# Attention steps split finer and each placed by hand, weights joined in four steps, and a reordered end, in a linear-attention and cosine-FFN kernel on one core

## The chip, the cores and the metric

The kernel runs on 1 core of one Trainium2 chip. The metric is device microseconds of one execution. Before the change the median of 3 runs is 587.07 us (585.82 to 587.1). Five engines work side by side, each in the order of its own instruction list: PE (matmuls, with the weight load PEld), DVE (elementwise, scans), ACT (activations), POOL (elementwise) and SP (issues transfers).

## The reference, cut to what matters

Two stages follow each other: a linear attention with decay over 768 steps, for 4 batches and 8 heads of 48, and a feed-forward stage on its output, seen as 3072 tokens of 384.

```python
for t in range(S):                         # attention, per batch and head
    cur = u * kt (outer) vt
    y[t] = rt @ (state + cur)
    state = wt[:, None] * state + kt (outer) vt
x = y as (B*S, H*D)                        # 3072 x 384
h = x @ w_in                               # 384 -> 2048
g = h * cos(h)
out = g @ w_out                            # 2048 -> 384
```

## The kernel before, in words

The time axis is cut into chunks of 128 steps, each of two halves of 64 (SUB); 4 batches of 6 chunks are 24 chunks (`j`), and two chunks of different batches form a block (BLK = 2), so there are 12 blocks. Attention in a chunk is done with matmuls: scores inside a half, a state carried from half to half.

The steps of a chunk or block, by the short names of the tables (before's lines):
- `load`, `lr`, `lv` (L195 to L214) issue the transfers of the transposed tile `tt` (112 x 1545: r, k, and the decays w), of `rk` and of `v`.
- `decay` (L216) is one step: `rkt` for the first six chunks, the suffix scan `ee` (L223), the running minimum `shrink` (L226), `whole` (L228), its reciprocal into `inj` (L229), the prefix scan into `tt` (L230), and r and k scaled by the two (L233, L234).
- `diag` (L236) makes `cd` and, on the engine that the table names for `asb`, the diagonal of the score tile (L255).
- `a`/`A` (L269) scores and the masked copy (L281), `t`/`T` (L283) transposes of k and the copy to `kn`, `s` (L303) states, `d` (L264) decayed states `dd`, `o` and `b` (L336) the own part of the output, `p` (L359) the past part, the copy `yf` and the transfers `xf<-yf` that turn the layout, `x` (L379) the split of `xf` into a high part (a cast) and a low part (a subtraction) `xT`.

The feed-forward runs in units: a block has 8 units of 256 hidden columns, 96 in all. `mm1` (L419) is 18 matmuls into a PSUM bank `ph`, then `gate` (L395): ACT L399, DVE L400, ACT L401 (sine) and L402 (square), DVE L403, then the cast `gh` to `gs` and two low parts `g0`, `g1` (L155). L403 is the last reader of the bank. `mm2` (L436) is 12 matmuls into the block's accumulators, up to LAG = 3 units behind mm1; after a block's last unit `ob` (L454) goes out.

Weights come as 64-bit words; `load_weights` (L164) makes a float from the two halves of a word and splits it into a high and a low part: ACT L174 and L176, DVE L178, L179 and L186, ACT the cast, DVE the low part (L155). This is done once for 16 pieces, during the first units.

What sets the order: `START` (L60) is a written list of steps up to block 2 with the units of blocks 0 and 1 between, `PLAN` (L52) the list that each later unit adds, 8 rows for the 8 units of a block; PE follows these lists as written. The other engines' order comes from a scheduler that goes by program order and its own costs. `EARLY` and `LATER` say which engine does what (v DVE, a ACT, p POOL, s SP). After the last unit a `vote` (L570) sums two checks in PSUM, every engine loads its result (L582), and a branch skips the fallback `one_by_one`.

## Time and profile before

| | us |
|---|---|
| median of the runs (3) | 587.07 |
| lowest, highest | 585.82, 587.1 |
| the profiled execution's own time | 586.22 |
| its span, first to last instruction | 584.5 |
| PE busy | 514.9 |
| DVE busy | 415.9 |
| ACT busy | 258.5 |
| POOL busy | 241.7 |
| mean granted TensorE clock | 0.977 of 2.4 GHz |

A busy time is the time in which at least one instruction of the engine ran. An engine takes its instructions in order, so an instruction that waits holds back all behind it. A releaser is what ended such a wait. PE is the busiest engine; its idle time shows in which stage another engine or a transfer sets the pace.

### The profile page before, as it was taken

The numbers are of one execution on the slowest core, as the hardware profiler recorded it, in microseconds if no ns is written. First come the engines' busy times: TensorE is split into PE (matmuls) and PEld (weight loads), VectorE is DVE, ScalarE is ACT, GpSimd is POOL, SyncE is SP. The second block draws the span as 40 slices with busy tenths as digits, with TensorE's granted clock in tenths as the row PEclk, the third lists the DMA queues.
The fourth block names the chain that finished last, engine by engine and source line by source line (L and its number), as shares of the span: only waits on it lengthen the run. The fifth ranks groups of instructions, "written<-read, shape, count | busy, mean of one in ns | idle before, by whom it ended". The sixth has DMA issues, their size and how long they took to land.

```text
span 584.5 us, 14459 instructions
## 1 busy us (share of the span) xinstructions
PE 514.9 (88%) x6084; PEld 489.4 (84%) x6084; DVE 415.9 (71%) x716; ACT 258.5 (44%) x445; POOL 241.7 (41%) x280
## 2 busy tenths in 40 slices
PE   1557588988889999899899999899899899999994
PEld 1447478877878989899899989899799899999994
DVE  6998999999586874964963965855854846945431
ACT  2435678843354253253353453353442443443541
POOL 2221443565445445453543635534543533243231
PEclk9999879999899999999999999999999899999998
DMA  8928354002432504305205207006015006401001
GB/s 280 333 68 295 113 181 153 24 33 82 138 105 93 130 2 144 88 29 148 58 29 150 56 29 192 13 29 178 1 32 148 1 28 194 160 31 27 27 1 34
DMA packets 21849, 56.37 MB, mean 96 GB/s; under 512 B 3088, under 2 KB 13968, under 8 KB 21776
## 3 DMA queue, kind: packets, MB, share of 16 engines
q1 hardware_dynamic: 19616, 53.59, 30.6%
q10 hardware_dynamic: 2160, 1.77, 1.4%
q8 instruction: 50, 0.82, 0.6%
q14 instruction: 23, 0.19, 0.1%
HBM read 45.91 MB, written 4.72 MB: 87 GB/s over the span
## 4 chain that ended last, share of the span: by engine, by line
PE 47%; DVE 34%; DMA 10%; issue 4%; ACT 2%; SPq 1%; POOL 1%; DVEq 0%; ACTq 0%
PE acc L445 21%; PE ph L431 19%; DMA xf<-yf 5%; DVE tt L230 5%; DVE ee L223 4%; DMA tt<-tr 3%; DVE rr L403 3%; DVE w L155 2%; DVE rr L400 2%; DVE h L179 2%; PE py L348 2%; DVE h L186 2%; PE py L367 2%; DVE shrink L226 2%; DVE h L178 1%
## 5 line engine op out<-in xcount | busy, mean ns | idle before, releaser
L155 POOL TENSOR_TENSOR gs<-rr,gs 128x256 fp32r<-128x256 f32 x192 | 164.5, 878 | 254.2 <-DVE gs L152 186.5
L431 PE MATMUL ph<-xT,w 128*128 128x256 f32 x1728 | 229.5, 288 | 23.4 <-DVE rr L403 14.6
L431 PEld LDWEIGHTS ph<-xT,w 128*128 128x128 f32 x1728 | 219.5, 194 | 28.9 <-issue 15.7
L445 PE MATMUL acc<-w,gs 128*128 128x384 f32 x1152 | 221.5, 343 | 5.4 <-ACT gs L152 3.6
L445 PEld LDWEIGHTS acc<-w,gs 128*128 128x128 f32 x1152 | 198.2, 189 | 9.7 <-ACT gs L152 4.0
L401 ACT ACTIVATE rr<-rr 128x512 f32<-128x512 f32 x96 | 60.7, 632 | 162.7 <-DVE rr L400 162.6
L400 DVE SCALAR_TENSOR_TENSOR rr<-rr,ph 128x512 f32<-128x512 int32 x96 | 65.1, 678 | 49.0 <-ACT rr L399 49.0
L403 DVE SCALAR_TENSOR_TENSOR rr<-rr,ph 128x512 f32<-128x512 f32 x96 | 65.4, 682 | 41.0 <-ACT rr L402 39.9
L399 ACT ACTIVATE rr<-ph 128x512 int32<-128x512 f32 x96 | 56.8, 591 | 82.0 <-PE ph L431 68.6
L402 ACT ACTIVATE rr<-rr 128x512 f32<-128x512 f32 x96 | 60.6, 632 | 2.6
L223 DVE TENSOR_TENSOR_SCAN ee<-tt,one_e 112x520 f32<-112x520 f32 x24 | 35.3, 1472 | 24.9 <-DMA tt<-tr 24.9
L152 DVE CAST gs<-rr 128x512 fp32r<-128x512 f32 x79 | 33.8, 428 | 6.5 <-PE acc L445 5.4
L255 POOL TENSOR_TENSOR asb<-cd,diag 128x512 f32<-128x512 f32 x24 | 27.6, 1151 | 23.8 <-ACT cd L152 12.2
L233 POOL TENSOR_TENSOR tt<-tt 112x512 f32<-112x512 f32 x18 | 22.3, 1241 | 30.4 <-DVE tt L230 30.4
L230 DVE TENSOR_TENSOR_SCAN tt<-tt,inj 112x520 f32<-112x520 f32 x24 | 33.5, 1395 | 0.2
L152 ACT CAST w<-h 128x768 fp32r<-128x768 f32 x16 | 13.3, 833 | 24.7 <-DVE h L186 24.7
L348 PE MATMUL py<-asb,v 64*64 64x64 f32 (+1 forms) x768 | 18.6, 232 | 5.5 <-DVE settled L354 2.1
L348 PEld LDWEIGHTS py<-asb,v 64*64 64x64 f32 (+1 forms) x768 | 14.8, 135 | 9.5 <-DVE settled L354 2.5
L245 DVE TENSOR_TENSOR rk<-rk 128x384 f32<-128x384 f32 x18 | 12.9, 717 | 12.2 <-DMA rk<-tn 12.1
L277 PE MATMUL pa<-tt 48*64 48x64 f32 x768 | 17.7, 242 | 3.5 <-DVE tt L233 1.9
L277 PEld LDWEIGHTS pa<-tt 48*64 48x64 f32 x768 | 15.3, 152 | 6.0 <-ACT xT L152 2.0
L291 PE MATMUL pt<-ident,tt 48*128 48x48 f32 (+1 forms) x192 | 10.6, 239 | 9.5 <-POOL tt L234 9.4
(72 smaller groups left out, 400.8 us busy)
## 6 DMA issues: line engine op xcount, KB each, us to landing
tt<-tr SPq DMA_DIRECT2D x24, 675.9 KB, 7.1
raw<-wts SPq DMA_DIRECT2D x16, 768.0 KB, 7.1
rk<-tn SPq DMA_DIRECT2D x18, 384.0 KB, 3.4
v<-tn SPq DMA_DIRECT2D x24, 192.0 KB, 3.2
out<-ob SPq DMA_DIRECT2D x24, 192.0 KB, 2.0
ww<-w SPq DMA_DIRECT2D x6, 768.0 KB, 4.4
xf<-yf SPq DMA_DIRECT2D x15, 144.0 KB, 5.0
xf<-yf ACTq DMA_DIRECT2D x9, 144.0 KB, 6.3
```

What stands on the lines that cost most here:

```text
L152: (nc.scalar.copy if E[name] is nc.scalar else E[name].tensor_copy)(out=out, in_=in_)
L155: E[name].tensor_tensor(out=out, in0=full, in1=high.bitcast(F32), op=ALU.subtract)
L223: nc.vector.tensor_tensor_scan(out=ee.rearrange("p a t -> p (a t)")[:, ::-1], data0=wp[:, 1:W65 + 1][:, ::-1], data1=one_e.rearrange("p a ...
L230: nc.vector.tensor_tensor_scan(out=wp[:, 0:W65], data0=wp[:, 0:W65], data1=inj.rearrange("p a t -> p (a t)"), initial=0.0, op0=ALU.mult, o ...
L348: nc.tensor.matmul(out=outs[i][SWAPPED[p]][ROW * o:ROW * o + m, n, p // 2, subs(q)], lhsT=a["v"][subs(q), head_cols(p, h, m)], rhs=a["asb" ...
L399: nc.scalar.activation(nn, ph, AF.Copy, scale=INV2PI / W_SCALE)
L400: nc.vector.scalar_tensor_tensor(out=rr, in0=nn, scalar=-2.0 * math.pi * W_SCALE, in1=ph, op0=ALU.mult, op1=ALU.add)
L401: nc.scalar.activation(rr, rr, AF.Sin, scale=0.5 / W_SCALE)
L402: nc.scalar.activation(rr, rr, AF.Square)
L403: nc.vector.scalar_tensor_tensor(out=rr, in0=rr, scalar=-0.5, in1=ph, op0=ALU.add, op1=ALU.mult)
L431: nc.tensor.matmul(out=ph[:, fi], lhsT=wgt[u * FU + fi][:, 0, a, kt * 128:(kt + 1) * 128], rhs=xT[:, b, kt], start=n == 0, stop=n == 3 * K ...
L445: nc.tensor.matmul(out=accs[i][j][:, :DM], lhsT=gs[:, a, fi, j * C:(j + 1) * C], rhs=wgt[u * FU + fi][:, 1, b], start=u == 0 and fi == 0 a ...
```

## The change

`decay` is split into `u` (rkt), `e` (suffix scan and `whole`, now written to `kept`, one column for each chunk), `k`, `q` (reciprocal, prefix scan) and `r`; `shrink` goes, its check is made once at the vote on all of `kept`. `diag` is split into `diag` (cd) and `i` (asb), the scores into `a` and `m` (the masked copy), `x` into `x` (high) and `l` (low). Weights are fetched (`f`), read by ACT (`h`), joined (`w`) and split (`y`) in four placed steps. The gate ends in `end_gates` (L403, cast, low parts before), which the sign `g` places and mm2 makes sure of. The first two tiles come in three transfers, the decays first. Engines that change: in EARLY `kn` and `g1` go to DVE; in LATER `asb` and `dd` go from POOL to DVE, `xh` from DVE to ACT, and half of the `xf` transfers from ACT's queue to SP's. The vote stands two units before the end; the last unit's mm2 finishes one chunk, then the other, and the last rows go out in halves from two engines and two queues. The fallback handles all batches in one loop instead of four.

```diff
+SPLIT = 2
-HP = 50
-EARLY = dict(asb="p", ..., k3="p", ..., kn="a", dd="v", ..., g0="p", g1="p", x="v", ...)
-LATER = dict(asb="p", gh="v", yf="a", xh="v", ..., kn="a", dd="p", ..., qx0="s", qx1="a", qo="s")
+HP = 100
+VOTE = 2
+EARLY = dict(asb="p", ..., k3="p", ..., kn="v", dd="v", g0="p", g1="v", x="v", ...)
+LATER = dict(asb="v", gh="v", yf="a", xh="a", ..., kn="a", dd="v", ..., qx0="s", qx1="s", qo="s")
-PLAN = ["T+1 mm2 mm1",
-        "mm1 A+1 mm2 decay+4",
...
-        "p+1 mm1 mm2 load+6 lv+6 load+7 lr+7",
-        "mm2 mm1 x+2 lv+7",
+PLAN = ["g mm2 T+1 mm1 e+4",
+        "mm1 g u+4 A+1 mm2 k+4 q+4 q+5",
...
+        "p+1 x+2 mm1 load+6 d+4 g mm2 lr+7",
+        "g lv+6 mm2 mm1 lv+7 lr+6 l+2",
...
+START = ["r0 lv0 u0 f q0 load1 f e0 diag0 diag1 k0 i0 t0 w i1 f h s0 m0 o0 k2 load0 t1 q2 b0 m1 f a1",
...
-    mask = cst.tile([C, NP, SUB], U8, name="mask")
+    mask = cst.tile([C, SUB], U8, name="mask")
...
-    def load_weights(f):
+    def high_words(f):
...
+        h = buf("h", [128, 2, DM], I32)
+        nc.scalar.activation(h.bitcast(F32), hi.bitcast(F32), AF.Copy, scale=2.0 ** -111)
...
+    def join_words(f):
...
+    def low_words(f):
...
-        E["qt"].dma_start(out=tt, in_=tr[g])
+        if j < SPLIT:
+            for lo, hi in ((1024, 1025 + W65), (512, 1024), (0, 512)):
+                E["qt"].dma_start(out=tt[:, lo:hi], in_=tr[g, :, lo:hi])
+        else:
+            E["qt"].dma_start(out=tt, in_=tr[g])
...
-        nc.vector.tensor_tensor(out=shrink, in0=shrink, in1=ee[:, :, 0], op=ALU.min)
-        a["whole"] = whole = buf("whole", [R, NS], F32)
+        a["whole"] = kept[:, a["j"]]
+        nc.vector.tensor_single_scalar(out=a["whole"], in_=ee[:, :, 0], scalar=LEAST, op=ALU.max)
+
+    def att_k(a):
+        E["k3"].tensor_tensor(out=a["k3"], in0=a["k3"], in1=a["ee"][:, :, 1:SUB + 1], op=ALU.mult)
+
+    def att_prefix(a):
...
-        units[t] = gate(sb, ph)
+        gates[t] = gate(sb, ph)
+
+    def end_gates(t):
+        for n in sorted(gates):
+            if n <= t:
+                units[n] = gate_end(sb, *gates.pop(n))
...
+        end_gates(t)
         gs = units.pop(t)
...
+        closing = t == slots - 1
+        for group in [(j,) for j in range(BLK)] if closing else [tuple(range(BLK))]:
...
+                    if closing and j == BLK - 1:
+                        half = DM // 2
+                        nc.scalar.activation(ob[:, :half], accs[i][j][:, :half], AF.Copy, scale=-2.0 / W_SCALE ** 2)
+                        nc.scalar.dma_start(out=rows_out[:, :half], in_=ob[:, :half])
+                        nc.vector.tensor_scalar(out=ob[:, half:], in0=accs[i][j][:, half:DM], scalar1=-2.0 / W_SCALE ** 2, scalar2=None,
+                                                op0=ALU.mult)
+                        nc.sync.dma_start(out=rows_out[:, half:], in_=ob[:, half:])
...
         elif n == 1 and up1[1] < up1[0]:
+            if up1[1] == slots - VOTE:
+                bad.append(vote())
             mm2(up1[1])
...
-            if t >= slots - NU + 2 and n_checked[0] < WCH:
+            if t >= slots - NU - 2 and n_checked[0] < WCH:
```

How this moves the lists, at three places. First DVE at its start, from the first tile's work on. Before:

```order
L220 TENSOR_TENSOR rkt<-tt 112x512
L223 SCALAR_TENSOR_TENSOR ee<-tt,one_e 112x520
L226 TENSOR_TENSOR shrink<-shrink,ee 112x8
L228 TENSOR_SCALAR whole<-ee 112x8
L229 RECIPROCAL inj<-whole 112x8
L230 SCALAR_TENSOR_TENSOR tt<-tt,inj 112x520
L233 TENSOR_TENSOR tt<-tt 112x512
```

And in the changed kernel:

```order
L241 SCALAR_TENSOR_TENSOR ee<-tt,one_e 112x520
L245 TENSOR_SCALAR kept<-ee 112x8
L252 RECIPROCAL inj<-kept 112x8
L253 SCALAR_TENSOR_TENSOR tt<-tt,inj 112x520
L235 TENSOR_TENSOR rkt<-tt 112x512
L258 TENSOR_TENSOR tt<-tt 112x512
```

The two scans, which need the decays alone, now stand ahead of the work on r and k; the row of `shrink` is gone.

Second DVE at the boundary between two blocks of the steady part, from the first `ee` of the next block's decays (`rr<-rr,ph` are the gate's two DVE steps, L400 then L403 before, L435 then L441 now). Before:

```order
L223 SCALAR_TENSOR_TENSOR ee<-tt,one_e 112x520
L400 SCALAR_TENSOR_TENSOR rr<-rr,ph 128x512
...
L403 SCALAR_TENSOR_TENSOR rr<-rr,ph 128x512
...
L229 RECIPROCAL inj<-whole 112x8
L223 SCALAR_TENSOR_TENSOR ee<-tt,one_e 112x520
L230 SCALAR_TENSOR_TENSOR tt<-tt,inj 112x520
L400 SCALAR_TENSOR_TENSOR rr<-rr,ph 128x512
L226 TENSOR_TENSOR shrink<-shrink,ee 112x8
...
L245 TENSOR_TENSOR rk<-rk 128x384
L230 SCALAR_TENSOR_TENSOR tt<-tt,inj 112x520
L403 SCALAR_TENSOR_TENSOR rr<-rr,ph 128x512
```

And in the changed kernel:

```order
L435 SCALAR_TENSOR_TENSOR rr<-rr,ph 128x512
L241 SCALAR_TENSOR_TENSOR ee<-tt,one_e 112x520
L245 TENSOR_SCALAR kept<-ee 112x8
L248 TENSOR_TENSOR tt<-tt,ee 112x512
L156 CAST gs<-rr 128x512
L441 SCALAR_TENSOR_TENSOR rr<-rr,ph 128x512
L252 RECIPROCAL inj<-kept 112x8
L253 SCALAR_TENSOR_TENSOR tt<-tt,inj 112x520
L156 CAST gs<-rr 128x512
L159 TENSOR_TENSOR xT<-xf,xT 128x3x128 x2
L435 SCALAR_TENSOR_TENSOR rr<-rr,ph 128x512
...
```

A gate's first step now stands ahead of the scan that needs the next tile, one scan instead of two or three lies between a gate's two steps, and the casts of `xT` are no longer in this list.

Third PE at its end (`acc<-w,gs` is the last unit's mm2, `pv` the vote; the numbers after `w_` tell the pieces of weights). Before:

```order
L575 MATMUL pv<-ones,vote 1x1
L576 MATMUL pv<-low,ones 1x8
```

stand after all of mm2. In the changed kernel:

```order
L622 MATMUL pv<-ones,fast_w 1x1
L623 MATMUL pv<-low,ones 1x1
L491 MATMUL acc<-w_1169,gs 128x384 x2
L491 MATMUL acc<-w_1302,gs 128x384 x2
...
L491 MATMUL acc<-w_1357,gs 128x384
L491 MATMUL acc<-w_1366,gs 128x384
...
```

The vote lies ahead of the last two units, and the last unit's rows come one at a time (x2 no more): six for one chunk, then six for the other.

## Rows read from the trace of the kernel before

**Rows 1.** Part 1 of the page: busy us of each engine, share of the span, instructions.
```profile
PE 514.9 (88%) x6084; PEld 489.4 (84%) x6084; DVE 415.9 (71%) x716; ACT 258.5 (44%) x445; POOL 241.7 (41%) x280
```

**Rows 2.** Busy time by stretch: the stretch, its length, busy us (x instructions) of PE, PEld, DVE, ACT, POOL, then the granted clock, DMA share, GB/s.
```profile
0.00:50.80 50.80, 22.59 (x353) 19.46 (x353) 45.20 (x78) 18.01 (x32) 13.04 (x16) 1.00 0.74 235
50.80:84.00 33.20, 24.81 (x304) 22.32 (x304) 30.93 (x46) 22.59 (x34) 9.65 (x7) 0.85 0.59 181
84.00:147.00 63.00, 54.37 (x510) 51.08 (x511) 62.81 (x88) 39.88 (x68) 32.90 (x27) 0.97 0.24 78
147.00:204.70 57.70, 53.48 (x679) 50.23 (x680) 41.86 (x75) 23.80 (x43) 26.52 (x31) 0.97 0.42 118
204.70:500.00 295.30, 282.53 (x3512) 270.67 (x3511) 196.27 (x364) 120.78 (x214) 132.94 (x162) 0.99 0.29 80
500.00:576.90 76.90, 76.90 (x728) 75.55 (x726) 38.56 (x67) 32.61 (x58) 26.63 (x38) 1.00 0.11 36
```

**Rows 3.** Who PE waited for from 204.7 to 500 us: us in total, times, longest (the longest of the list).
```profile
PE ph L431 <- DVE rr L403: 11.1, 6, 2.4
```

**Rows 4.** ACT in order of time at one block boundary: start, us, instruction, in brackets the idle time before it and its releaser.
```profile
231.89 0.60 ACT L399 ACTIVATE rr<-ph 128x512 int32<-128x512 f32 x1 [1.66 <-POOL dd L262]
...
238.17 0.58 ACT L399 ACTIVATE rr<-ph 128x512 int32<-128x512 f32 x1
...
245.42 0.63 ACT L402 ACTIVATE rr<-rr 128x512 f32<-128x512 f32 x1
```

**Rows 5.** DVE in order of time at the same boundary.
```profile
235.11 1.24 DVE L223 TENSOR_TENSOR_SCAN ee<-tt,one_e 112x520 f32<-112x520 f32 x1 [2.61 <-DMA tt<-tr]
236.27 0.66 DVE L400 SCALAR_TENSOR_TENSOR rr<-rr,ph 128x512 f32<-128x512 int32 x1
...
237.95 1.01 DVE L152 CAST xT<-xf 128x384 fp32r<-128x384 f32 x2
238.87 0.68 DVE L403 SCALAR_TENSOR_TENSOR rr<-rr,ph 128x512 f32<-128x512 f32 x1
...
240.27 0.56 DVE L155 TENSOR_TENSOR xT<-xf,xT 128x384 fp32r<-128x384 f32 x1
...
244.07 0.66 DVE L400 SCALAR_TENSOR_TENSOR rr<-rr,ph 128x512 f32<-128x512 int32 x1
...
247.72 0.66 DVE L403 SCALAR_TENSOR_TENSOR rr<-rr,ph 128x512 f32<-128x512 f32 x1
```

**Rows 6.** PE in order of time there (matmuls in a row are one line; ends overlap).
```profile
244.49 2.28 PE L431 MATMUL ph<-xT,w 128*128 128x256 f32 x18
248.53 1.65 PE L431 MATMUL ph<-xT,w 128*128 128x256 f32 x12 [1.76 <-DVE rr L403]
```

**Rows 7.** DVE in order of time at the start.
```profile
5.40 0.69 DVE L220 TENSOR_TENSOR rkt<-tt 112x512 f32<-112x512 f32 x1 [3.31 <-DMA tt<-tr]
6.01 1.24 DVE L223 TENSOR_TENSOR_SCAN ee<-tt,one_e 112x520 f32<-112x520 f32 x1
...
7.36 1.16 DVE L228 TENSOR_SCALAR whole<-ee 112x8 f32<-112x8 f32 x1
...
11.28 1.44 DVE L116 CAST mask<-maskf 64x256 uint8<-64x256 f32 x2
```

**Rows 8.** The list of transfers, one line of it: KB each, median us from issue to landing.
```profile
out<-ob SPq DMA_DIRECT2D x24, 192.0 KB, 2.0
```

**Rows 9.** Durations in ns, min/median/max, with first and last start, from the answers on single tiles.
```profile
L155 POOL TENSOR_TENSOR gs<-rr,gs x192: 726/739/2181, 60.3 to 574.1; 128x256 fp32r<-128x256 f32 x192
L262 DVE TENSOR_TENSOR dd<-sn,whole x4: 305/326/892, 34.7 to 120.3; 112x192 f32<-112x192 f32 x4
L155 DVE TENSOR_TENSOR xT<-xf,xT x24: 546/551/1537, 49.7 to 531.4; 128x384 fp32r<-128x384 f32 x24
L152 ACT CAST xT<-xf x6: 496/516/527, 47.5 to 163.1; 128x384 fp32r<-128x384 f32 x6
L226 DVE TENSOR_TENSOR shrink<-shrink,ee x24: 141/172/1178, 7.3 to 457.0; 112x8 f32<-112x8 f32 x24
L179 DVE SCALAR_TENSOR_TENSOR h<-raw,sign_bit,h x16: 1001/1007/1800, 13.3 to 124.1; 128x768 int32<-128x768 int32 x16
```

**Rows 10.** Groups of instructions by shape: total busy, mean ns | idle before, releaser.
```profile
L226 DVE TENSOR_TENSOR shrink<-shrink,ee 112x8 f32<-112x8 f32 x24 | 10.8, 448 | 0.1
L179 DVE SCALAR_TENSOR_TENSOR h<-raw,sign_bit,h 128x768 int32<-128x768 int32 x16 | 18.6, 1161 | 0.1
```

**Rows 11.** Who PE waited for from 49 to 204.7 us, the three longest.
```profile
PE acc L445 <- ACT gs L152: 3.6, 2, 2.6
PE ph L431 <- DVE rr L403: 3.5, 3, 2.0
PE ph L431 <- DVE w L155: 3.1, 2, 2.3
```

**Rows 12.** The last work on ACT.
```profile
576.85 0.87 ACT L454 ACTIVATE ob<-acc 128x384 f32<-128x384 f32 x2 [4.97 <-PE acc L445]
```

**Rows 13.** SP's queue in order of time, around one block's turn of layout and at the end: start, us, transfers issued.
```profile
230.25 0.61 SPq L376 DMA_DIRECT2D xf<-yf  x1
230.91 2.66 SPq L333 DMA_DIRECT2D xf<-yf  x2
...
577.37 0.81 SPq L456 DMA_DIRECT2D out<-ob  x2
```

More of the change, by code (lines that the diff above doesn't have):

```diff
@@ L137, in rwkv_cos_ffn @@
     nc.vector.memset(three, 3)
-    raw, wgt, last = {}, {}, {}
+    raw, wgt, last, parts = {}, {}, {}, {}
     E = {}
@@ L440, in mm2 @@
             accs[i] = [ps.tile([C, 512], F32, tag=x, name="acc") for x in tags]
+        end_gates(t)
         gs = units.pop(t)
-        for a, b in PASSES:
-            for fi in range(FU):
-                for j in range(BLK):
-                    nc.tensor.matmul(out=accs[i][j][:, :DM], lhsT=gs[:, a, fi, j * C:(j + 1) * C],
-                                     rhs=wgt[u * FU + fi][:, 1, b],
-                                     start=u == 0 and fi == 0 and a == 0 and b == 0, stop=u == NU - 1 and fi == FU - 1 and a == 1)
@@ L495, in att @@
             att(j, "s")
+            for c in range(j * BLK, (j + 1) * BLK):
+                att(c, "m")
+        elif n == "m":
+            if (i, "A") not in seen:
+                att(j, "a")
+            if "pa" not in atts[j]:
+                seen.add((j, n))
+                return
+            for c in atts[j]["pa"][0]:
+                att(c["j"], "i")
         seen.add((j, n))
@@ L532, in events @@
                     up(1)
+            elif e == "g":
+                if gates:
+                    end_gates(min(gates))
             else:
@@ L542, in slot, with vote @@
         events(i, PLAN[n], t)
-    up1 = [0, 0]
+    def vote():
+        fast_w = cst.tile([128, 1], F32, name="fast_w")
+        nc.vector.tensor_single_scalar(out=fast_w, in_=wmax, scalar=1.0, op=ALU.is_gt)
+        small = buf("ee", [R, NG, NS], F32, "small")
+        nc.vector.tensor_single_scalar(out=small, in_=kept, scalar=LEAST, op=ALU.is_le)
+        low = cst.tile([R, 1], F32, name="low")
+        nc.vector.tensor_reduce(out=low, in_=small.rearrange("p j a -> p (j a)"), axis=mybir.AxisListType.X, op=ALU.add)
+        pv = bank("a", [C, 512], "pv")
+        nc.tensor.matmul(out=pv[:1, 0:1], lhsT=fast_w, rhs=ones[:, 0:1], start=True, stop=True)
+        nc.tensor.matmul(out=pv[:1, 1:2], lhsT=ones[:R, 0:1], rhs=low, start=True, stop=True)
+        votes = cst.tile([1, 1], F32, name="votes")
+        nc.vector.tensor_reduce(out=votes, in_=pv[:1, 0:2], axis=mybir.AxisListType.X, op=ALU.add)
+        bad = cst.tile([1, 1], I32, name="bad")
+        nc.vector.tensor_copy(out=bad, in_=votes)
+        return bad
+    up1, bad = [0, 0], []
     engines(EARLY)
```

258 lines of the change are left out of this document (135 added, 123 removed), and 11 rows, old and new, of the table START.

## The prediction

> **What bounds the kernel now.** I read the busy times first, then the table by stretch, then the list of PE's waits, then single boundaries in order of time. PE is busy 514.9 us and DVE 415.9 us [rows 1]; the reader is to see that a mean says little here, since the bound changes with the stage [rows 2]. Up to 147 us DVE is the bound: it has work for 62.81 of the 63 us from 84 to 147 and for 30.93 of the 33.2 before, and for 45.20 of the first 50.8, most of the rest being the wait for the first tile. PE has its first dense work at 50.8 us and from there to 84 it is busy 24.81 of 33.2 us, at a granted clock of 0.85, so part of that time at the lower level of 1.2 GHz. From 147 on DVE has slack (41.86 of 57.7, then 196.27 of 295.3 us), and PE is near its own limit: 282.53 of 295.3 us from 204.7 to 500, and all of 76.9 us after that. What is to be had is therefore the start, the 12.8 us in which PE idles between 204.7 and 500, the 4.2 us from 147 to 204.7, and the end. The last part before the end, 500 to 576.9, offers nothing.
>
> The list of waits says what the 12.8 us are: 11.1 us, 6 times, for L403, the second DVE step of the gate, which frees the bank that the next mm1 writes [rows 3]. At one boundary the cause can be followed. ACT has L399 ready at 232.5 us [rows 4], but DVE, in order, stands at the scan `ee` until the next tile lands at 235.11, and so does L400 only at 236.27 and L403 at 238.87 [rows 5]. The next gate fares worse: ACT is done at 238.75 [rows 4], L400 comes at 244.07, behind the low parts of xT, another `ee` and a prefix scan; ACT's square is done at 246.05 [rows 4], L403 comes at 247.72 [rows 5]. PE had finished its matmuls at 246.77 and goes on at 248.53, after 1.76 us [rows 6]. So it is the order of DVE's list, not DVE's amount of work, that PE waits for in the steady part.
>
> **The first tile.** The scans need 521 of the tile's 1545 columns. Before, `rkt` starts when the whole tile has landed, at 5.40, and `ee` at 6.01 [rows 7]. Now the decays come first. They land no later than 5.40; the earliest that a transfer asked for at the start could land I put at 2.8 (issued at 0.8, and 2.0 us to landing, the least in the list of transfers [rows 8]). I take the middle, 4.1, so `ee` starts 1.9 us earlier, 0.6 of it because `rkt` goes behind. The mask loses three quarters of its columns: of 1.44 us [rows 7] about 1.0 goes. `shrink` gives 0.2 for each of two tiles (median 0.172 [rows 9]). Against it stand four copies `kn` on DVE; the nearest row is an operation of 192 columns, 0.33 us [rows 9], so 1.3. Sum: -1.9 -1.0 -0.4 +1.3 = **-2**, bounds -4 (all of it a microsecond better, ACT relieved of `kn`) and +1 (landing at 5.40, `kn` behind other work).
>
> **The start from 50.8 to 147.** DVE is full here, so every microsecond on its list counts. Added: 16 low parts `g1` of 256 columns, between 0.33 us at 192 columns and 0.55 at 384 [rows 9], by columns 0.40, so 6.4; the other 8 copies `kn`, 2.6. Removed: four more `shrink` at the mean of 0.448 [rows 10], 1.8. Net +7.2. Relief: POOL loses those 16 at 0.739 [rows 9], 11.8 of its 42.6 us in the two stretches [rows 2]. DVE's L179 takes 1.161 in the mean and 1.007 in the median [rows 9, 10], 15% more, and I see such stretching where POOL runs: `whole`, 8 columns wide, took 1.16 us at 7.36 [rows 7]. If 15% of DVE's 93.7 us is stretch and goes with POOL's work, 28% of 14 is -3.9. Left is +3.3. The finer steps work the other way: PE's waits on weights and gates of 3.6, 3.5 and 3.1 us [rows 11] come from an order in which all of a weight's or chunk's work is placed at once. I take -3.3 for that, a third of those 10.2, so **0**; bounds -10 (all three waits) and +7.2 (no relief, no better order).
>
> The Trainium skill, SBUF — State Buffer, section Who interferes with whom, says that a DVE instruction with two SBUF inputs and a POOL instruction that reads SBUF block each other fully, the later one waiting for the earlier. The stretched rows agree with it. The operations that this change moves to DVE all have two inputs there, so by that rule they would be blocked in their turn; half a POOL operation for each of the 16 would be +6, an estimate, and this term would come out at the far end of its bounds.
>
> **The steady part.** DVE gains, for each block, two `asb` of 512 columns (0.68 us, as L403 in [rows 5]) and four `dd` (0.33 [rows 9]) and loses two casts of xT (1.01 together [rows 5]) and two `shrink` (0.9 [rows 10]): +0.8 us on an engine with 99 us of slack in seven blocks, which hides it. ACT takes the two casts at 0.516 [rows 9]; it is busy 120.8 of 295.3 us. Now I set the new order against the same times. L435 goes ahead of the scan and runs at 232.5. The scan starts at 235.11, and with `kept`, k and a cast (0.16, 0.69, 0.42) L441 runs at 237.6, not 238.87. Then come a reciprocal, the prefix scan, a cast, and the low parts of xT. For these the transfers must have landed, before at about 237.9; half of them move from ACT's queue to SP's, three issues at about 0.63, so 1.9 later: 239.8 less what they had to spare, say 239.4. ACT's two casts end at 240.4, the low parts at 241.5 (before 240.83). ACT's first step of the next gate stands behind the casts, ends at 241.0, L435 runs at 241.5, then one scan, `kept` and k, and L441 ends its wait at 244.3, where PE needs it at 246.8. The bank is free 2.5 us too early instead of 1.8 us too late. I take all of the waits for L403, **-11.1**, and leave the other 1.7 us. Bounds: -12.8, and 0 where another wait comes in its place.
>
> From 147 to 204.7 the same cause holds for part of PE's 4.2 idle us; I take half, **-2**, bounds 0 and -4.
>
> **The end.** PE ends at 576.8; ACT's two copies take 0.87 us [rows 12], SP issues two transfers from 577.37 to 578.18 [rows 13]. Now one chunk's rows leave while PE works at the other, the last copy is half as wide and the two halves are issued side by side: -0.4 for the second issue, -0.3 for the copy. The vote leaves the end, but it ended at 577.5, ahead of SP, and hid behind it. The 6.3 us after 578.18, in which the last transfer lands and the branch is taken, I leave. **-0.8**, bounds 0 and -2.
>
> **Sum.** 586.22 - 2 - 0 - 11.1 - 2 - 0.8 = 570.3 for the profiled execution's own time, which stands 0.85 below the median shown, so about **571 us** for the median, 2.7% less. Less than 0.3%, 1.8 us, cannot be told from no change.
>
> **The rivals.** (1) DVE's debt: the start takes +7.2 and gets nothing back, while the rest comes as forecast: 571 + 7.2 = 578. For it speaks that DVE is full to 147 us; against it that POOL has 28% less to do there. With the sentence on the rule above it would be 584. (2) The waits move: DVE's list is shorter at the boundary, but PE then waits for something else, for example the score copy, whose asb is now on DVE too. Then the steady term is 0, and the time 571 + 11.1 = 582. Against it: the 2.5 us of slack worked out above. (3) Slower: the turn of layout. All six `xf` issues now stand in SP's queue, ACT's casts wait for them, and behind the casts wait the next gate's ACT steps. The low parts end at 241.5 and PE first reads them at 244.49 [rows 6], so it decides at 3.0 us: if the transfers land more than that later, PE stops once in each block. Two issues on SP have taken 2.66 us together [rows 13]; if all six go at that pace, 8.0 us instead of the 3.3 of before, xT is 4.7 late and not 1.9, and, counting from 240.83 and one chunk's scan, `kept` and k (2.1) ahead of it on DVE, ends at 247.6, 3.1 after PE wants it. The gate behind the casts costs some of the same time again, say 0.9. Ten blocks at 4.0 are +40 at worst; at half that pace +20, and 571 + 20 = 591, slower than before. For it: the transfers' landing is on the chain already. Against it: 3.0 us of slack, and issues that took 0.6 us where nothing held SP. (4) The three transfers do not bring the decays earlier: +2 and 573, inside the range.
>
> **How the numbers follow.** Forecast, with its bounds on single terms, 0.62; rival 1 0.13; rival 2 0.12; rival 3 0.09; a little of everything that leaves the time where it was 0.04. The likeliest case's own range is 561 to 577. To hold the time 8 times in 10, the range takes in rivals 1 and 2 on the upper side, to 584, and on the lower side more of the start's waits, to 558. Faster by over 0.3%: 0.62 + 0.13 + 0.12 = 0.87, less 0.02 for rival 2 with a bad start, so 0.85; within 0.3%: 0.05; slower: 0.10.
>
> **What would show it.** Right: in the list of PE's waits from about 200 us to the last block, L441 is near zero where L403 had 11.1; PE's first dense ph some 2 us earlier; DVE still full to about 145 us and POOL busy less there; two transfers issued side by side after the last matmul. Wrong: a new line of some microseconds for each block in PE's waits, on xT (rival 3) or on the score copy (rival 2); first mm1 later than 51 us; or PE idle for gs or w between 85 and 150 us more than before (rival 1).

## The result and the profile after

The changed kernel takes 561.24 us in the median of four executions; one of the four was disturbed, and without it the median is 560.34 (558.99 to 562.13). Against the kernel before, measured beside it at 586.45, the ratio is 0.956 (95% interval 0.952 to 0.960): 4.4% less. The forecast was 571, its range 558 to 584. The profiled execution took 558.99 us, with a span of 557.1, against 586.22 and 584.5 before.

Part 1 of the page after, which answers to [rows 1]: PE is busy for 2 us less, DVE for 24 more, POOL for 42 less.

```profile
PE 512.7 (92%) x6084; PEld 488.4 (88%) x6084; DVE 440.2 (79%) x754; ACT 264.6 (48%) x450; POOL 200.1 (36%) x214
```

The table by stretch after, to be read beside [rows 2]: stretch, length, busy us of PE, PEld, DVE, ACT, POOL, granted clock, DMA share, GB/s.

```profile
0.00:48.60 48.60, 22.57 (x353) 19.58 (x353) 43.52 (x79) 16.12 (x24) 14.46 (x16) 1.00 0.85 242
48.60:82.00 33.40, 27.04 (x317) 25.36 (x317) 30.43 (x48) 24.45 (x36) 3.92 (x4) 0.85 0.68 222
82.00:140.00 58.00, 53.21 (x512) 50.69 (x511) 57.81 (x95) 39.12 (x63) 17.17 (x16) 1.00 0.13 42
140.00:194.00 54.00, 51.08 (x663) 47.86 (x663) 51.04 (x92) 22.39 (x41) 19.00 (x18) 0.97 0.51 148
194.00:475.00 281.00, 280.24 (x3504) 268.30 (x3505) 217.21 (x374) 128.10 (x226) 120.18 (x127) 1.00 0.29 82
475.00:553.60 78.60, 78.54 (x748) 76.63 (x746) 39.83 (x71) 34.14 (x59) 25.38 (x35) 1.00 0.13 41
```

The stretches of this table are cut by time and do not hold quite the same work as those of [rows 2]; the terms below go by units. DVE is still full to 140 us. In the steady part PE now idles 0.8 us of 281, where it was 12.8 of 295.3. The list of PE's waits from 190 to 480 us, which answers to [rows 3], has one line left, and it is not the gate's second DVE step (L441, formerly L403):

```profile
PE acc L491 <- POOL gs L159: 0.8, 2, 0.4
```

To put the gain in its places I use the 96 units (one mm1 and its gate each). ACT's first step of a gate starts when PE has finished that unit's mm1, so its start in the order of time dates the unit. The table gives, in us, when unit 1 is reached, the stretches between units, and what lies from unit 96 to the end of the span; all kernels of the study are in it, under the letters of the experiments below. Each row is one execution.

```
kernel                        unit 1   1 to 16  16 to 24  24 to 80  80 to 96  96 to end    span
before                         54.85    100.21     49.22    290.78     74.08      15.36   584.5
after                          52.68     95.41     44.50    279.37     73.28      11.86   557.1
a  xf's second queue back      52.58     93.88     48.92    292.66     73.01      11.95   573.0
b  before, that queue alone    55.38     99.61     47.93    282.96     72.84      15.58   574.3
c  steady steps whole          53.11     95.12     49.58    277.88     73.85      11.96   561.5
d  first tiles whole           54.14     95.95     47.07    280.36     73.59      12.19   563.3
e  start's engines back        53.46     99.46     53.39    278.65     73.95      11.89   570.8
f  start's weights whole       55.53     94.91     51.90    278.78     74.00      11.98   567.1
g  start's chunk steps whole   51.79    102.44     54.48    278.70     74.00      11.89   573.3
h  vote last                   52.66     95.45     45.46    280.70     74.00      12.33   560.6
j  before, new fallback        55.35     99.48     48.20    292.57     74.08      14.12   583.8
k  all low parts on DVE        52.41     93.10     52.33    280.69     73.88      11.99   564.4
l  sign by ACT                 52.88     94.47     51.42    278.65     73.89      11.89   563.2
m  k, and three buffers rk     51.86     94.12     49.92    279.42     73.42      11.86   560.6
```

After against before, term by term: -2.2, -4.8, -4.7, -11.4, -0.8, -3.5, together -27.4. From 24 to 80 the ten kernels that have this queue and the changed steps lie between 277.9 and 280.7, so differences of 1 to 2 us in a stretch say little. Up to 178 us the kernels after, a, c and h have the same order of instructions on DVE, ACT and POOL, and still unit 16 starts up to 1.6 us apart in them and unit 17 up to 4.4. The row of after is the fastest execution of its kernel, 1.35 us below the median, that of c the slowest, 3.4 above it. Up to unit 24, differences of that size between two rows are therefore neither gain nor loss by themselves.

The boundary of [rows 5] after, DVE in order of time (two scans `ee`, with L435 and L441 where L400 and L403 were):

```profile
221.55 0.68 DVE L435 SCALAR_TENSOR_TENSOR rr<-rr,ph 128x512 f32<-128x512 int32 x1
224.14 1.24 DVE L241 TENSOR_TENSOR_SCAN ee<-tt,one_e 112x520 f32<-112x520 f32 x1 [1.91 <-DMA tt<-tr]
...
226.44 0.68 DVE L441 SCALAR_TENSOR_TENSOR rr<-rr,ph 128x512 f32<-128x512 f32 x1
...
228.75 3.27 DVE L159 TENSOR_TENSOR xT<-xf,xT 128x384 fp32r<-128x384 f32 x2
231.94 0.67 DVE L435 SCALAR_TENSOR_TENSOR rr<-rr,ph 128x512 f32<-128x512 int32 x1
...
234.49 0.68 DVE L441 SCALAR_TENSOR_TENSOR rr<-rr,ph 128x512 f32<-128x512 f32 x1
```

The scan still waits for its tile, 1.91 us, but the gate's step L435 is now ahead of it in DVE's list and no longer waits with it. The second gate's L441 ends at 235.17, and PE does not stop for it:

```profile
233.68 2.53 PE L469 MATMUL ph<-xT,w 128*128 128x256 f32 x19
```

A unit is 18 matmuls. The 19th of this row, at 235.93, is the first of the next unit and the first that writes the bank which this L441 frees (three units later, as in [rows 5, 6]). It has 0.76 us to spare; at the next six boundaries the margin is 0.76 to 4.6 us.

### The profile page after: what moved, and what is told of

It is laid out like the page before. It is cut to its first block, busy times and chain, and to the rows that moved or that the text cites. A ratio compares the mean times of both kernels' runs of the same rounds, so it can differ in the third digit from the quotient of the medians.

```text
span 557.1 us, 14381 instructions
## 1 busy us (share of the span) xinstructions
PE 512.7 (92%) x6084; PEld 488.4 (88%) x6084; DVE 440.2 (79%) x754; ACT 264.6 (48%) x450; POOL 200.1 (36%) x214
## 5 line engine op out<-in xcount | busy, mean ns | idle before, releaser
L159 POOL TENSOR_TENSOR gs<-rr,gs 128x256 fp32r<-128x256 f32 x176 | 156.2, 907 | 305.4 <-DVE gs L156 213.0
L469 PE MATMUL ph<-xT,w 128*128 128x256 f32 x1728 | 226.7, 287 | 5.7 <-ACT w L156 2.6
L469 PEld LDWEIGHTS ph<-xT,w 128*128 128x128 f32 x1728 | 216.1, 191 | 9.4 <-ACT w L156 2.8
L491 PEld LDWEIGHTS acc<-w,gs 128*128 128x128 f32 x1152 | 201.2, 190 | 4.9 <-POOL gs L159 2.1
L435 DVE SCALAR_TENSOR_TENSOR rr<-rr,ph 128x512 f32<-128x512 int32 x96 | 65.4, 681 | 45.5 <-ACT rr L434 45.0
L434 ACT ACTIVATE rr<-ph 128x512 int32<-128x512 f32 x96 | 57.1, 595 | 90.6 <-PE ph L469 86.5
L441 DVE SCALAR_TENSOR_TENSOR rr<-rr,ph 128x512 f32<-128x512 f32 x96 | 65.3, 681 | 28.8 <-ACT rr L437 27.2
L241 DVE TENSOR_TENSOR_SCAN ee<-tt,one_e 112x520 f32<-112x520 f32 x24 | 29.6, 1233 | 12.9 <-DMA tt<-tr 12.9
L159 DVE TENSOR_TENSOR xT<-xf,xT 128x384 fp32r<-128x384 f32 x24 | 30.8, 1320 | 0.2 <-ACT xT L156 0.2
L258 POOL TENSOR_TENSOR tt<-tt 112x512 f32<-112x512 f32 x18 | 24.9, 1386 | 7.8 <-DVE tt L253 7.8
L264 PE MATMUL pc<-u_by_head,rkt 112*128 112x2 f32 x48 | 9.4, 317 | 15.6 <-DVE rkt L235 14.2
L264 PEld LDWEIGHTS pc<-u_by_head,rkt 112*128 112x128 f32 x48 | 9.1, 282 | 16.1 <-DVE rkt L235 14.2
L174 ACT ACTIVATE h<-raw 128x768 f32<-128x768 f32 x16 | 14.6, 914 | 16.5 <-DVE w L159 13.9
## 6 DMA issues: line engine op xcount, KB each, us to landing
xf<-yf SPq DMA_DIRECT2D x24, 144.0 KB, 3.3
```

Of the source, the lines that this page charges most:

```text
L159: E[name].tensor_tensor(out=out, in0=full, in1=high.bitcast(F32), op=ALU.subtract)
L434: nc.scalar.activation(nn, ph, AF.Copy, scale=INV2PI / W_SCALE)
L435: nc.vector.scalar_tensor_tensor(out=rr, in0=nn, scalar=-2.0 * math.pi * W_SCALE, in1=ph, op0=ALU.mult, op1=ALU.add)
L441: nc.vector.scalar_tensor_tensor(out=rr, in0=rr, scalar=-0.5, in1=ph, op0=ALU.add, op1=ALU.mult)
L469: nc.tensor.matmul(out=ph[:, fi], lhsT=wgt[u * FU + fi][:, 0, a, kt * 128:(kt + 1) * 128], rhs=xT[:, b, kt], start=n == 0, stop=n == 3 * K ...
L491: nc.tensor.matmul(out=accs[i][j][:, :DM], lhsT=gs[:, a, fi, j * C:(j + 1) * C], rhs=wgt[u * FU + fi][:, 1, b], start=u == 0 and fi == 0 a ...
```

## The experiments

Each kernel was timed beside the kernel before; ratios are to that. The kernel after has 0.956 (0.952 to 0.960).

**a and b: one letter.** By the printed order of DVE's list, one entry of the table LATER changes that order at the boundaries: `qx1`, the queue on which half of the transfers of xf are issued. Two kernels test it from both sides; the other entries were not run alone.

```diff
 # a: the changed kernel, in LATER
-qx1="s"
+qx1="a"
 # b: the kernel before, in LATER
-qx1="a"
+qx1="s"
```

> The changed kernel with one letter back as it was: in LATER, the transfers of the second head's rows of xf are issued by ACT again (qx1="a"), all else as changed. In this order DVE has the scan ee ahead of L435 at each block's boundary again and the low parts of xT on either side of the cast gs, as in the kernel before. Theory A, the queue of these transfers decides DVE's order at the boundary and with it the 11 us: PE's waits for L441 from 190 to 480 us come back, 6 to 12 us, and the time is 567 to 573. Theory B, the finer steps and their places removed those waits: the waits stay under 2 us and the time is 559 to 563. Theory C, six issues in SP's queue cost what rival 3 said, only less: shorter than 561 by 1 to 4 us.

> The kernel before with that one letter alone changed: in LATER, qx1="s" for qx1="a"; no step is split, no engine of an operation changed. DVE then has L399 and L400 of the boundary ahead of the scan ee, as the changed kernel has. Theory A: PE's waits for L403 from 204.7 to 500 us, 11.1 us before, fall to under 3, and the time to 574 to 579. Theory B: the waits stay at 9 to 12 us and the time at 585 to 588. Theory C: slower than before, 588 to 600, with waits on xT.

Measured: a 575.91 us, ratio 0.983 (0.978 to 0.987); b 574.03 us, 0.979 (0.974 to 0.984). Theory A holds in b, time and waits. In a it holds for the direction: the time is 3 us above its range, and the waits for L441 stay under theirs. One letter gives the kernel before 2.1%, and its loss takes 2.7 points from the changed one. In the table the stretch from 24 to 80 goes up by 13.3 in a and down by 7.8 in b. PE's waits from 190 to 480 us in a:

```profile
PE acc L491 <- POOL gs L159: 6.8, 9, 1.0
PE ph L469 <- DVE rr L441: 2.4, 4, 1.1
PE acc L491 <- DVE gs L156: 0.5, 2, 0.2
```

I had expected them all at L441; most moved one step on, to the gs that L441 leads to, so only the sum of 9.7 fits. The place is the old one. DVE and then ACT of run a at the boundary:

```profile
227.15 1.24 DVE L241 TENSOR_TENSOR_SCAN ee<-tt,one_e 112x520 f32<-112x520 f32 x1 [2.50 <-DMA tt<-tr]
228.31 0.66 DVE L435 SCALAR_TENSOR_TENSOR rr<-rr,ph 128x512 f32<-128x512 int32 x1
```

```profile
223.63 0.60 ACT L434 ACTIVATE rr<-ph 128x512 int32<-128x512 f32 x1 [1.80 <-PE ph L469]
229.01 0.63 ACT L436 ACTIVATE rr<-rr 128x512 f32<-128x512 f32 x1 [4.78 <-DVE rr L435]
```

ACT's first step is done at 224.2, L435 stands behind a scan that waits for DMA, and ACT idles 4.78 us: the picture of [rows 4, 5]. The letter also gives ACT its issues back, but they are not what holds the gate here: PE's mm1 ends at 223.05 and ACT's L434 starts at 223.63, while L435 comes 4.1 us after L434 has ended. In b the letter alone puts the step ahead of the scan:

```profile
231.00 0.68 DVE L400 SCALAR_TENSOR_TENSOR rr<-rr,ph 128x512 f32<-128x512 int32 x1
233.42 1.24 DVE L223 TENSOR_TENSOR_SCAN ee<-tt,one_e 112x520 f32<-112x520 f32 x1 [1.74 <-DMA tt<-tr]
```

PE's waits of b from 204.7 to 500 us, 11.1 for L403 before [rows 3], are now

```profile
PE ph L431 <- DVE rr L403: 2.6, 4, 0.9
PE ph L431 <- DVE inj L229: 1.6, 1, 1.6
PE pst L313 <- DVE asb L281: 1.3, 3, 0.8
```

The letter alone is worth 7.8 of the 11.4 us of this stretch. The other 3.6 come only together with the rest of the change; by c, below, not from the finer steps, which leaves the moved engines of LATER and the row of `shrink`. No run separates these.

**c: the steady part's steps whole again.**

```diff
-PLAN = ["g mm2 T+1 mm1 e+4", "mm1 g u+4 A+1 mm2 k+4 q+4 q+5", ...]
+PLAN = ["g mm2 T+1 mm1", "mm1 g A+1 m+2 mm2 u+4 e+4 q+4 r+4 k+4", ...]
         gates[t] = gate(sb, ph)
+        if later:
+            end_gates(t)
```

> The changed kernel with its steady part's steps whole again: after the start, all five decay steps of a chunk stand at one place in the plan, asb behind its diag, the mask copy behind the scores, the low part of xT behind its cast, and the gate's end behind its beginning. Queues and engines as changed. Theory A: nothing of the 11 us hangs on it; 559 to 564 us, waits for the gate from 190 to 480 us under 3 us. Theory B: the waits come back, 568 to 573 us.

Measured: 560.09 us, 0.956 (0.951 to 0.960); from 24 to 80 it needs 277.9 us, no more than after. Theory A. After the start, the finer steps and their places are worth nothing that can be measured.

**d: the first tiles in one transfer.**

```diff
-SPLIT = 2
+SPLIT = 0
```

> The changed kernel with the first two tiles fetched in one transfer each (SPLIT = 0). Theory A, the split brings the decays earlier and the start is a chain from there: the first ee starts 1 to 2 us later than 3.99 and the first unit's mm1 ends 1 to 2 us later than 52.68, the time 562 to 564. Rival: the first unit's time is set by DVE's other work, so ee later by as much moves it by less than 0.5 us; 561 to 562 us.

Measured: 563.16 us, 0.960 (0.956 to 0.965). DVE's first rows of run d, and the one of after:

```profile
5.76 0.69 DVE L235 TENSOR_TENSOR rkt<-tt 112x512 f32<-112x512 f32 x1 [3.69 <-DMA tt<-tr]
6.37 1.23 DVE L241 TENSOR_TENSOR_SCAN ee<-tt,one_e 112x520 f32<-112x520 f32 x1
```

```profile
3.99 1.24 DVE L241 TENSOR_TENSOR_SCAN ee<-tt,one_e 112x520 f32<-112x520 f32 x1 [1.91 <-DMA tt<-tr]
```

The scan is 2.38 us later, the first unit 1.46, and the units 4 to 16 are each 2.0 us later, within 0.3. Theory A. By these rows the three transfers are worth 1.5 us at the first unit and 2.0 behind it; the ratios alone, 0.960 and 0.956, overlap. By the 17th unit it is 4.7; the last section shows the same jump in c and what is behind it.

**e: the start's engines back.**

```diff
 # EARLY
-kn="v", ... g1="v"
+kn="a", ... g1="p"
```

> The changed kernel with the start's two moves to DVE undone: in EARLY, the copies kn are ACT's again and the low parts g1 POOL's (kn="a", g1="p"); the order of the steps is as changed. The time from the end of the first unit's mm1 to that of the 16th was 95.41 us in the kernel after, 100.21 before. Theory A, DVE is full here and the moves cost what the prediction counted, 3.3 us net, so that the finer order is worth some 8: that time falls to 91 to 94, the whole to 557 to 560. Theory B, relief of POOL is worth more than DVE's added work, so the moves are part of the gain: 97 to 101, the whole 562 to 567. Theory C, neither: within 1 us.

Measured: 571.55 us, 0.980 (0.975 to 0.984). Theory B: from unit 1 to 16 it takes 99.5 us. The whole is longer than theory B said, because another 8.9 us are lost from 16 to 24, part of that at a lower clock (0.51 granted from 160 to 170 us, 1.00 in after). The run undoes two moves at once and does not tell `kn` from `g1`. POOL's low parts between 50 and 147 us, of after and then of e (total us, mean ns):

```profile
L159 POOL TENSOR_TENSOR gs<-rr,gs 128x256 fp32r<-128x256 f32 x15 | 15.2, 1010 | 65.3 <-ACT gs L156 65.3
```

```profile
L159 POOL TENSOR_TENSOR gs<-rr,gs 128x256 fp32r<-128x256 f32 x27 | 35.0, 1315 | 51.7 <-ACT gs L156 48.8 <-DVE w L159 2.9
```

A gate's two low parts stand one behind the other on POOL, 2.6 us by this mean, where they were one on each engine; and while POOL runs, DVE's own operations are longer. In the same place of the two programs DVE has, of after and then of e, where POOL's work lies beside the first 0.7 us and beside all of it,

```profile
103.08 1.28 DVE L258 TENSOR_TENSOR tt<-tt 112x512 f32<-112x512 f32 x1
```

```profile
108.49 2.39 DVE L258 TENSOR_TENSOR tt<-tt 112x512 f32<-112x512 f32 x1
```

and the same operation at 10.00 us of run d, with POOL still, takes 0.69. How much of DVE's time that is can be seen from unit 1 to 16: stretch, length, busy us of PE, PEld, DVE, ACT, POOL, granted clock, DMA share, GB/s, of before, after and e.

```profile
54.85:155.06 100.21, 82.92 (x924) 76.71 (x925) 94.10 (x135) 64.16 (x104) 48.08 (x42) 0.91 0.33 104
52.68:148.09 95.41, 81.95 (x924) 77.57 (x925) 93.10 (x152) 65.27 (x103) 23.20 (x21) 0.93 0.35 113
53.46:152.92 99.46, 81.90 (x924) 76.78 (x925) 96.85 (x139) 64.14 (x104) 46.88 (x36) 0.95 0.39 112
```

With 13 operations fewer than in after, DVE is busy for 3.8 us more in e, and POOL for twice as long. DVE is full in both; the table under k divides its time.

**f and g: the start's places.** In f a weight's steps stand together where its low part stood; in g a chunk's.

```diff
 # f, in START
-"... f h s0 ... h h ... w ... y w y ..."
+"... f s0 ... h w y h w y ..."
 # g, in START
-"r0 lv0 u0 f q0 load1 f e0 diag0 diag1 k0 i0 t0 ..."
+"lv0 f load1 f u0 e0 q0 r0 k0 diag0 i0 diag1 i1 t0 ..."
```

> The changed kernel with a weight's steps of the start together again: what ACT, DVE and the low parts do for one weight stands at the place at which its low part stood, in place of three places apart. Theory A, the finer places of the weights are what made the start shorter: from the first unit to the 24th (139.91 us after, 149.43 before) some 3 to 8 us come back, and the whole is 564 to 570. Theory B, the scheduler puts DVE's and ACT's instructions by what is ready, so the place in the program matters little, as in the steady part: within 1.5 us, 560 to 563.

> The changed kernel with the chunks' steps of the start together again: bonus product, suffix scan, prefix scan, r and k of a chunk at one place, asb behind its diag, the mask copy behind its scores, the low part of xT behind its cast. The weights stay in four steps. Theory A: the chunk's finer steps made the start shorter: first unit 0 to 1 us later, and from the first to the 24th unit 3 to 8 us come back, the whole 564 to 570. Theory B: within 1.5 us, 560 to 563.

Measured: f 567.64 us, 0.973 (0.969 to 0.978); g 573.58 us, 0.983 (0.978 to 0.988). Theory A in f, though its stretch from unit 1 to 16 is no longer than in after: it loses 2.9 us at the first unit and the rest behind the 16th. In g only the direction is theory A's; the loss is twice its range, and the first unit comes 0.9 us sooner, not later. From unit 1 to 24, f gives back 6.9 us and g 17.0, e before it 12.9: 36.8 together, though the whole change gained only 9.5 there. The medians of the whole say the same, 7.3, 13.2 and 11.2 us. So these are not shares of the gain. In e and g the new list START with one part taken out is worse from unit 1 to 24 than the old list with all of them out (149.4 before, 152.9 in e, 156.9 in g), which speaks for a list that suits only the engines and steps it was written for.

**h and j: the end.** h moves the vote behind the last unit again; j gives the shorter fallback to the kernel before; no execution enters it.

```diff
 # h
-            if up1[1] == slots - VOTE:
-                bad.append(vote())
...
         while up1[1] < slots:
             up(1)
+    bad.append(vote())
 # j, in one_by_one
-        for b in range(NB):
-            with tc.For_i(0, S // C, 1) as i:
+        with tc.For_i(0, NG, 1) as i:
```

> The changed kernel with the vote at the end again, behind the last unit, its form as changed. From the end of PE's last acc matmul to the end of the span it was 3.6 us after, 7.7 before. Theory A, what follows the vote (each engine loads it and takes the branch) lay on the end and not behind SP's transfers, as the prediction had it: it becomes 6.5 to 8, and the whole 3 to 4 us longer than the kernel after. Theory B, the vote hides behind SP's transfers: 3.5 to 4.5, the whole within 1 us.

> The kernel before with the changed kernel's fallback, the code that the last branch jumps over: one loop over all chunks in place of a loop written out for each batch. Nothing that is executed changes. From the end of the last unit's mm1 to the end of the span it was 15.4 us before, 11.9 after, 12.3 with the vote last. Theory A, the shorter jump is what made the end shorter by some 3 us, since after the last transfer has landed the engines fetch code (the trace of before has instruction packets at 583 us, 4 us behind the last transfer): 12 to 13 us, the whole 582 to 584. Theory B, the halved last rows did it: 15 to 15.6, the whole 585 to 587.

Measured: h 561.60 us, 0.963 (0.959 to 0.968); j 585.84 us, 0.9995 (0.996 to 1.003). The vote's place is worth little in the trace (12.33 us from unit 96 to the end, 11.86 after): most of it hides, as theory B has it. The ratio, 0.7 points above that of after, cannot settle so small a difference; the intervals touch. The end of run h, first DVE, then SP:

```profile
556.59 0.14 DVE L625 CAST bad<-votes 1x1 int32<-1x1 f32 x1
```

```profile
557.04 0.33 SPq L506 DMA_DIRECT2D out<-ob  x1
```

The fallback gives 1.2 us in the trace (14.12, was 15.36), between the two theories and less than the comparison of times can tell; run b, with the old fallback, has 15.58. Behind SP's last issue lie 6.3 us before, 5.1 in j, 3.2 in h and 2.4 after, and from issue to landing the transfers take 1.6 to 2.2. Behind the last landing it is 4.7 before, 4.5 in b, 3.3 in j, 2.0 in h and 1.1 after. The Trainium skill, Runtime: NRT & Kernel Launch, section Instruction fetch mechanics, says that a taken branch to a target outside the fetched window makes the engine fetch code before it goes on. The traces fit it: before has instruction packets from 579.3 to 580.1 us and again from 582.85 to 583.2, some 3 us behind the last landing; in j the second group comes only at the very end of the span, and in after none lies between the last landing and the end. What such a fetch costs, no run here shows.

**k, l and m: is DVE's work the bound of the start?** k moves the other half of the start's low parts to DVE too; l takes a step from DVE and gives ACT two for six weights; m is k with one buffer more.

```diff
 # k, in EARLY
-g0="p"
+g0="v"
 # l
-BY_ACT = ()
+BY_ACT = (4, 6, 8, 10, 12, 14)
 # m: k, and in BUFS
-rk=2
+rk=3
```

> The changed kernel with the other half of the gate's low parts moved from POOL to DVE too, in the start alone (EARLY g0="v"). From 50 to 147 us these are 15 operations, 15.2 of POOL's 23.2 us. Theory A, POOL and DVE hold each other up when both read SBUF, so that an operation on POOL costs DVE as much as its own: DVE's added 15 at 0.42 are paid by what is no longer stretched, first to 24th unit 0 to 6 us shorter than 139.9, the whole 556 to 562. Theory B, DVE is full and each of them counts: 5 to 8 us longer, the whole 566 to 569.

> The changed kernel with BY_ACT = (4, 6, 8, 10, 12, 14): for six weights ACT makes the sign, in two more steps, and DVE's shift (0.59 us) falls away. ACT has 31 us free from 50 to 147. Theory A, DVE's work alone sets the start: first to 24th unit 2 to 3.5 us shorter than 139.9, the whole 557 to 560. Theory B, the two steps of some 0.9 us each stand on the weight's chain and ahead of a gate's steps on ACT: 0 to 5 us longer, 561 to 567.

Measured: k 564.29 us, 0.964 (0.960 to 0.968); l 564.77 us, 0.963 (0.959 to 0.968). By the whole, k lies between its two theories and l in theory B; by the time from unit 1 to 24, 145.4 and 145.9 us, both come out on theory B's side. The intervals of k and l overlap that of h, so the whole does not settle a loss of 2 to 4 us.

From unit 1 to 16, k is 2.3 us and l 0.9 us shorter than after. The second is within what kernels with the same lists differ by there (1.6), and the first hardly beyond it; besides, in k six operations of DVE, 3.7 us of work, come behind unit 16 that came ahead of it in after. So neither run makes that stretch shorter beyond doubt. What k does show is that 15 low parts more on DVE, 0.415 us each, do not make it longer. DVE stays full:

```profile
52.41:145.51 93.10, 81.25 (x923) 77.01 (x924) 90.24 (x161) 65.41 (x103) 9.26 (x6) 0.95 0.36 113
```

DVE's time from unit 1 to 16 can be divided. As own work I count each operation at a duration that only a tenth of its kind (same operation, tiles and shape, all traces) stays under; the rest of its time is stretch. These are estimates from the traces; neighbouring operations overlap a little, so the parts add up to more than the length.

```
kernel  length  own work  stretch  beside POOL  DVE idle  POOL busy
before   100.2      86.9     16.5         16.2       6.1       48.1
after     95.4      95.2      8.5          7.9       2.3       23.2
e         99.5      90.8     15.7         15.3       2.6       46.9
k         93.1      97.7      4.4          2.8       2.9        9.3
l         94.5      93.7      9.0          8.2       2.3       25.0
```

Most of the stretch lies in operations that ran beside one of POOL's, and that part is about a third of POOL's busy time in every row (0.31 to 0.34). So DVE is the bound of this stretch, but its undisturbed work alone does not set the time: the hold by POOL counts with it. In l the 3.5 us taken off (six times 0.59) show as 1.5 less work, because four operations of a later chunk moved up.

From 16 to 24 k loses 7.8 us against the kernel after: the late work falls there, and from 150 to 160 us its granted clock is 0.83. Of these, 4.3 come from the 22nd to the 24th. SP and DVE of run k at that place:

```profile
176.15 3.30 SPq L226 DMA_DIRECT2D rk<-tn  x2
179.54 1.25 SPq L216 DMA_DIRECT2D tt<-tr  x1
```

```profile
188.17 1.24 DVE L241 TENSOR_TENSOR_SCAN ee<-tt,one_e 112x520 f32<-112x520 f32 x1 [3.59 <-DMA tt<-tr]
```

Two issues for rk wait for their buffers, the tile stands behind them in SP's queue, the scan waits for the tile, and the gate's second step stands behind the scan.

> The kernel with all low parts of the start on DVE (run k) and one change more: three buffers rk in place of two. In run k SP stands from 176.15 to 179.45 us at an issue for rk, which waits for its buffer, and issues the tile tt behind it only at 179.54; DVE's scan ee waits 3.59 us for that tile, and the units fall back by 4.3 us from the 22nd to the 24th. Theory A, this queue is the reason: with a third buffer the tile is issued 2 to 3 us earlier, DVE's wait falls under 1 us, first to 24th unit is 140 to 142 us in place of 145.4, the whole 558 to 561. Theory B, the tile waits for something else (its own buffer, or DVE's list is late anyway): 144 to 146 us, the whole 563 to 566.

Measured: 562.41 us, 0.960 (0.957 to 0.963). The same rows of run m:

```profile
176.79 1.65 SPq L226 DMA_DIRECT2D rk<-tn  x2
178.53 0.38 SPq L216 DMA_DIRECT2D tt<-tr  x1
```

```profile
186.22 1.24 DVE L241 TENSOR_TENSOR_SCAN ee<-tt,one_e 112x520 f32<-112x520 f32 x1 [1.67 <-DMA tt<-tr]
```

The tile is issued 1.0 us earlier, not 2 to 3; the wait halves, and units 1 to 24 take 144.0 us, 1.4 less than in k, which is theory B's range. The whole lies between the two theories. So the queue is part of the wait, but that it is the reason for the 4.3 us is not shown. Neither kernel beats the changed one.

## Why the prediction was right, and where it was not

**The steady part, -11.1, measured -11.4.** The mechanism was right: the gate's steps came out from behind the waiting scan, and PE's waits at the boundaries went. The size was right with less room than I had worked out: the bank is free 0.76 us ahead of PE at the boundary shown, not 2.5, above all because the two low parts of xT took 3.27 us together where I had 1.1. What I did not see is which part of the change does it. I worked with the changed order as a whole, and charged the queue's move to it as a cost (the transfers 1.9 us later). Runs a to c show that this move is what changes the order: alone it gives the old kernel 7.8 us, without it the new one has the waits again, and the split steps with their places add nothing here. So the move that I booked as a cost is most of the gain. Why the scheduler orders DVE's list otherwise when these transfers are on SP, no run shows.

**Rival 3, the same queue as the danger,** had a price of up to 40 us and came to nothing. SP did issue all six, from 218.75 to 223.11 us, and ACT's casts of xT still ran at 225.5, ahead of need. The low parts of xT took 1.32 us in the mean over the whole kernel, not the 0.56 that I had read (0.55 where POOL is still), and even that was covered.

**The first tile, -2, measured -2.2** at the first unit, of which the transfers are 1.5 by run d. The scan starts at 3.99 where I had 4.1; that was the middle of two bounds, so the hit is luck. The mask gave 0.3 us (1.44, now 1.14) and not 1.0. The sum came out right with parts that did not.

**The start to 147 us, 0, measured -4.8** between units 1 and 16. The kind of sum was right: DVE is nearly full there before and after. The step that failed is one of its terms, the relief by POOL. In the division under k, added work is +8.3, where I had +7.2; DVE's idle time fell by 3.8, where I had taken 3.3 for the better order, a third of three waits, which was a guess; but the stretch fell by 8.0, where I had 3.9. (The three make -3.5; the other 1.3 are overlaps of neighbouring operations.) I had the whole stretch nearly right, 14 us (16.5 in the table), and took too small a share of it away. That share, 28%, came from pricing POOL's low parts at the undisturbed 0.739. In the trace of before the 26 of them between 50 and 147 us took 1.25 in the mean, and POOL's busy time from unit 1 to 16 fell by half, from 48.1 to 23.2 us. Run e shows the other side: with the low parts back on POOL the stretch is back (15.7).

The rule that I weighed, in the Trainium skill, SBUF — State Buffer, section Who interferes with whom, gives a lock between POOL and a DVE operation with two SBUF inputs. I used one side of it only. The low parts moved to DVE are held up in their turn, 0.57 us in the mean in after against 0.415 in k, where POOL has none in the start; that is 2.5 us for 16, not 6. But by the same rule each operation taken off POOL ends a hold on DVE, and this is the larger part. The rows of e and k fit the lock. Two of my readings did not: the copies `kn` read PSUM and have no two SBUF inputs, and `whole`, which I named as a stretched row, has one.

**From 147 to 204.7, -2, measured -4.7** between units 16 and 24. The direction holds; some of it is clock, 1.00 from 148 to 195 us in this trace and 0.92 in that of c, which is no slower (last section). Run a, without the new order, has a clock of 1.00 there too and needs 48.9 us, of 49.2 before. Since c, of the same time as after, needs 49.6, how much of the 4.7 is gain is not shown.

**The end, -0.8, measured -3.5.** That the vote hides behind SP was mostly right: h changes 0.5. Wrong was to leave the 6.3 us behind the last issue as they were: the whole term lies behind the last landing, 4.7 us before and 1.1 after. By j the shorter fallback is 1.4 of these 3.6, by h the vote's place 0.9; some 1.4 stay without a cause. The halves, which I did price, gave 0.3 (from PE's last matmul to the last landing 2.8 us before, 2.5 after), and PE took 0.45 longer from unit 96 to its last matmul, which cancels them.

Rival 1 did not come (the start became shorter), nor rival 2 (what is left to PE is 0.8 us), nor rival 4 (run d). Of the 11 us by which the forecast was too long, the start is 4.8, the end 2.7 and the stretch after the start 2.7; no other term is off by 1.

## What to carry to other kernels

When an in-order engine has an operation in its list that waits for a transfer, see what stands behind it: here the 11 us hung on whether one gate step came ahead of one scan, and one letter, the queue of another transfer, decided most of that. Where a scheduler sets the order, print it for each part of a change alone; the part that moves the order is the part to price. And the busy time of an engine is not its work: here 8 us more work on DVE cost nothing, because moving it there halved POOL's time and with it the hold on DVE. Price the engine that is relieved at what its operations take beside the other, not at their undisturbed time.

## What the runs showed of the hardware

POOL and DVE slow each other beyond what I had allowed. POOL's low part of 256 columns took 0.73 to 0.75 us wherever none of DVE's two-input operations ran beside it (76 times in before), up to 2.18 otherwise, and 1.3 in the mean of run e from 50 to 147 us; DVE's product of 512 columns took 0.69 with POOL still, up to 2.39 beside it. From unit 1 to 16 DVE lost about a third of POOL's busy time in each of five traces.

A tile that landed later went with a loss of three times its delay, most of it at a lower clock. The kernels after and c have the same list on DVE up to 178 us and differ only later. In c the tile was issued 0.5 us later (144.31, not 143.85) and took 6.7 us to land, not 5.4; why, the traces do not show. So the scan `ee` of about 150 us waited for its tile in c, and in after it did not; DVE of after, then of c:

```profile
149.32 1.23 DVE L241 TENSOR_TENSOR_SCAN ee<-tt,one_e 112x520 f32<-112x520 f32 x1
```

```profile
151.06 1.24 DVE L241 TENSOR_TENSOR_SCAN ee<-tt,one_e 112x520 f32<-112x520 f32 x1 [1.51 <-DMA tt<-tr]
```

PE then waited for the gate behind it, 0.46 us in after and 1.77 in c. From 130 to 140 us it had been busy 6.9 and 6.8 of 10 us, and from 140 to 150 the granted clock was 0.83 in both, part of the time at 1.2 GHz. The next mm1, of after, then of c:

```profile
156.20 2.29 PE L469 MATMUL ph<-xT,w 128*128 128x256 f32 x17
```

```profile
159.20 3.71 PE L469 MATMUL ph<-xT,w 128*128 128x256 f32 x17
```

The same 17 matmuls take 1.4 us more in c: the lower level lasted longer there, 0.78 in the mean from 150 to 160 us where after has 1.00. PE's wait (1.3 us more) and what the clock lacks from 150 to 170 us (0.22 and 0.12 of ten us each, 3.4) are 4.7 together. From unit 16 to 24 it is 49.6 us against 44.5, which a reader of those two traces alone would put down to the changed plan. The times of the two kernels, 560.09 and 560.34, say otherwise: a stretch where PE pauses needs several executions before it is believed.
